# A fused attention and FFN kernel on one core: ten products of a cleared tile at the head of TensorE's order, and a new table of offsets for the order

## The chip, the cores and the metric

The kernel runs on one core of one Trainium2 chip. The metric is the device time of one execution in microseconds (us), the median of three runs. A core has TensorE (matrix products into the eight banks of PSUM), VectorE, ScalarE, GpSimd and SyncE, which here does nothing but issue DMAs. Each engine takes its instructions in the order in which the program lists them; semaphores hold an instruction until what it needs is there. In rows, PE is TensorE, PEld its weight loads, DVE VectorE, ACT ScalarE, POOL GpSimd, SPq SyncE's queue.

## What is computed

```python
def _attn_ref(q, k, v):                       # 8 batches, 12 heads, 448 positions, 64 columns
    scores = scale * np.matmul(q, k.transpose(0, 1, 3, 2)) - np.log(S)
    attn = 1.0 / (1.0 + np.exp(-scores))      # a sigmoid, no softmax
    return np.matmul(attn, v)

def _moe_ref(x, U, V, w_ch1, w_ch2):          # x: 8 x 448 x 768
    h = x.transpose(0, 2, 1) @ U @ V          # mixing over positions, rank 32
    u = x + h.transpose(0, 2, 1)
    ch = np.maximum(u @ w_ch1, 0.0) @ w_ch2   # 768 -> 3072 -> 768
    return u + ch
```

q, k and v are float32; U, V, w_ch1 and w_ch2 arrive as 64-bit floats and are decoded on the chip.

## The kernel before

**Stages.** Heads are taken in pairs, six pairs p per batch b. For each pair `S{b}{p}` on TensorE is a step of scores, ScalarE makes the sigmoid, `V{b}{p}` is the product with v, VectorE copies it out. After pairs 3 and 5, a half of the mixing follows: `M{b}{h}` (scale, split into two fp16 parts, transposes, product with U) and `N{b}{h}` (product with V, added to x, maximum of each row). `P{b}` splits u into two fp16 parts. The 64-bit weights come in pieces of 768 KB: `D{i}{g}` loads and decodes the four pieces of group g of matrix i (VectorE shifts and ors, ScalarE takes absolute sums), `E{i}{g}` splits them into two fp16 parts, `w__90` and the like. The FFN of batches 0 and 1 is plain: `I{b}{g}{f}` is one bank of 18 products of w1 with u, `O{b}{g}{e}` 12 products of w2. Batches 2 to 7 go in pairs by seven products of quarter matrices (`X`, `Y`, line L1209), whose sums `Q`, `R`, `T` are made ahead of time while the plain FFN runs. Float32 products stand for scores and values of most batches and cost two records each in the trace.

**What sets the order.** No instruction is placed by hand. Every step is recorded in a `Plan` with its engine, an assumed cost, what it reads and writes, the buffers that it needs and a position. `Plan.order` then goes through assumed time: of the steps that an engine could start, the one with the least position is next. Positions are worked out from some thirty constants (`START`, `ROOM`, `LEAD`, ...), and `SHIFT` has an offset for each group of steps and engine: `S13` moves the scores of pair 3 of batch 1, `L13s` their loads on SyncE (the trailing s). The program then has each engine's steps in that order. So a new number in `SHIFT` can move a step on its engine past any other that it doesn't depend on. Positions set the order alone; what a step waits for on the chip is set by semaphores.

**Names at the start.** `qk__99`, `qk__100` and `qk__101` hold q and k of a pair (two halves of 64 partitions each, so four loads), `v__102` to `v__105` hold v. `w` in a load from `w_in` is a piece of 64-bit weights. `junk` is a tile that ScalarE's absolute sums write to. The scores' line is L637 (L641 for the quarter of the positions that two pairs share, the quad tile), values L656 and L666, the load helper L460.

Of the kernel before, what the change touches and what calls it, by code (L numbers as in the profile page):

```python
# [71 lines left out]
MIX_2, EV_IN, EV_OUT, A_OFF = 4.517, 103.098, 7.053, -86.824
START, DECODE = 429.303, 176.054
U_AT, U_STEP = 18.398, 14.623
LEAD, SUMS, STEP_K, STEP_I, FFN_LEAD = -24.08, 276.154, 211.52, 183.044, -43.857
W_AT, W_STEP, PAIR0, MIX0A, MIX0B, W2_LAG, G0_LEAD = -168.245, 57.904, 30.158, 55.287, -54.095, 1.409, -15.896
LOW_G = 1
FB = 8
SHIFT = dict(
    mixing=-7.5, mixings=44.1, L00s=48.8, S00=92.2, V00=15.1, L01s=31, S01=63.5, V01=29.3, L02s=22.2, S02=45.5, V02=48.8, L03s=71.1, S03=90.8,  # L80
# [3 lines left out]
    D02=-10, E02=-11.3, E02s=-12.7, D12s=10.6, D12=31.3, E12=-11.2, E12s=-46.2, I020=33.2, O010=31.8, I021=6.4, O011=-35.7, I022=20.1, I023=14.7,
    O012=26, D03s=42.2, D03=28.2, E03=-30.4, E03s=20.9, D13s=-31.5, D13=-3.3, E13=13.4, E13s=-16, I030=48.6, O020=-73.1, I031=30.7, O021=-3.1,
    I032=36.4, I033=50, O022=16.1, D04s=-27.8, D04=1.2, E04=8.4, E04s=17.7, D14s=-59.4, D14=-19.9, E14=21, E14s=75.7, I040=-31.9, O030=-62.5,
    I041=-13, O031=-121.4, I042=-20.1, I043=22.8, O032=-110.2, D05s=-45.9, D05=13.7, E05=-54, E05s=-6.1, D15s=22.3, D15=15.2, E15=64.4, E15s=10,
    I050=2.9, O040=-70.1, I051=-25.7, O041=-77.1, I052=-55.7, I053=-67.8, O042=-96.4, L10s=87, S10=-28, V10=-47.5, L11s=59.7, S11=-18.1, V11=-16.8,
    L12s=79.5, S12=-26.7, V12=31.5, L13s=69.3, S13=-51.1, V13=41.4, M10=21.6, M10s=86.6, N10=-5.2, N10s=-56.2, L14s=51.6, S14=20.7, V14=16.7,
    L15s=80.7, S15=-15.9, V15=69.1, M11=14.1, M11s=185.1, N11=50.9, N11s=-94.5, P1=-23.4, P1s=5.3, L20s=94.9, S20=-29.9, V20=82.6, L21s=70.2,  # L90
    S21=11.8, V21=46.8, L22s=101.4, S22=-6.6, V22=79.8, L23s=112.5, S23=-11.3, V23=94.4, M20=24.5, M20s=-35.5, N20=-23.8, N20s=5.8, L24s=104.9,
    S24=-18.9, V24=95.2, L25s=108.1, S25=-11.6, V25=69.4, M21=-10.6, M21s=-39.5, N21=15.7, N21s=13.2, L30s=70.4, S30=-17.8, V30=-49.2, L31s=66.8,
    S31=2.2, V31=-47.6, L32s=92.9, S32=-6.8, V32=-107.6, L33s=79.2, S33=2.4, V33=-62.9, M30=17.4, M30s=-31.5, N30=33.9, N30s=-52.7, L34s=60.7,
    S34=-12.1, V34=-62.7, L35s=89.5, S35=-11.3, V35=-56.7, M31=-3.5, M31s=-77.6, N31=-8.3, N31s=6.3, L40s=71.9, S40=-21.7, S40s=-45.8, V40=60.4,
    L41s=61.1, S41=-21.5, S41s=-47.5, V41=85.2, L42s=83.1, S42=-27.8, S42s=-11, V42=45, L43s=76.9, S43=-21, S43s=-0.3, V43=31.2, M40=-2.5, M40s=-38.8,
    N40=14, N40s=5.2, L44s=56.8, S44=7.5, S44s=-21.3, V44=-23.3, L45s=93.6, S45=-6.8, S45s=3.5, V45=22.3, M41=-35.2, M41s=13.2, N41=16, N41s=-91.7,
    L50s=69.1, S50=-19.2, S50s=-17.3, V50=-61.5, L51s=78.6, S51=-40.2, S51s=-40.5, V51=-19.7, L52s=59.9, S52=-41, S52s=-26.2, V52=32.2, L53s=58.3,
    S53=-54.5, S53s=-12.6, V53=-13.7, M50=24.4, M50s=-31.2, N50=10.9, N50s=-20.7, L54s=50.5, S54=-1.2, S54s=-33.1, V54=-52.7, L55s=57.8, S55=-15.8,
    S55s=-47, V55=-57.8, M51=9.2, M51s=-35.7, N51=-30.8, N51s=34.5, L60s=-38.6, S60=-15.2, S60s=17.5, V60=31.7, L61s=22.4, S61=-1.9, S61s=5.6,
    V61=47.1, L62s=17.1, S62=-16.1, S62s=-12.5, V62=47.9, L63s=-15.4, S63=-19.7, S63s=-22.6, V63=43, M60=-38.9, M60s=59.8, N60=-2.5, N60s=-3.1,  # L100
    L64s=2.2, S64=-28.5, S64s=-22.4, V64=33.3, L65s=9.6, S65=2, S65s=-21.5, V65=58.6, M61=17, M61s=8.9, N61=27.9, N61s=-65.4, L70s=-27.4, S70=33.8,
    V70=6.9, L71s=-29.1, S71=22.1, V71=35.8, L72s=-49.3, S72=37.5, V72=42.5, L73s=-23.3, S73=34.4, V73=-19.4, M70=-39, M70s=-48.6, N70=8.2,
    N70s=-34.9, L74s=-6.2, S74=39, V74=35.5, L75s=-41.2, S75=54.5, V75=-1, M71=-85, M71s=-10.8, N71=18.9, N71s=-13.6, U1s=-69.2, U1=65.3, G1s=-57.1,
    F010s=6, F110s=-39.9, Q000=36.2, Q000s=-44.7, Q001=42.4, Q001s=-49.8, Q100=-52.3, Q100s=-58.6, Q101=-20.6, Q101s=33.5, I100=26.4, O050=-4.5,
    O050s=12.7, I101=-16.8, O051=-11.1, O051s=1.9, I102=3.3, I103=-13.2, O052=-17, O052s=-8.6, F011s=-4.2, F111s=5.3, Q010=17.8, Q010s=-55.8, Q011=11,
    Q011s=23.9, Q110=27.4, Q110s=31.2, Q111=-13.3, Q111s=23.3, I110=9.7, O100=10.9, I111=-56.7, O101=25.1, I112=-51.7, I113=-72.3, O102=34.3,
    F012s=83.4, F112s=-61.4, Q020=-20.6, Q020s=47.1, Q021=22.4, Q021s=49, Q120=3.6, Q120s=-35.8, Q121=-31.4, Q121s=-24.9, I120=-22.5, O110=40.2,
# [1366 lines left out]
```

## Time and profile before

| | us |
|---|---|
| median of three runs | 1526.42 |
| lowest and highest | 1525.07, 1526.78 |
| the profiled execution, own time | 1523.58 |
| its span, first to last instruction | 1521.8 |
| TensorE busy | 1504.0 |
| VectorE busy | 1072.8 |
| ScalarE busy | 668.1 |
| GpSimd busy | 301.3 |
| mean DMA rate | 199 GB/s |

The span is what rows are timed in, from its start. An engine's busy time is the union of its instructions; matmuls overlap in the records, so the sum of their durations is more than the time that they take. A wait is idle time of an engine in front of an instruction, with what ended it.

### The profile page before, as it was taken

What the parts mean: (1) busy time and instruction counts of PE and PEld (TensorE: products, weight loads), DVE (VectorE), ACT (ScalarE), POOL (GpSimd) and SP (SyncE); (2) the same over time, 40 slices, a digit from 0 to 9 for tenths busy, and PEclk for the clock granted to TensorE, in tenths of its full rate; (3) what the DMA queues carried; (4) which work ended last, traced back from release to release, by engine and by line L of the source; (5) the groups of instructions that cost most, each with busy time, mean ns of one, the idle gap of its engine ahead of it and who ended that gap; (6) DMA issues with size and microseconds to landing.
All of it is one profiled execution on the core that took longest, in us unless ns stands there. A gap on an engine that the chain in (4) does not pass through costs nothing.

```text
span 1521.8 us, 21953 instructions
## 1 busy us (share of the span) xinstructions
PE 1504.0 (99%) x8181; PEld 724.1 (48%) x8181; DVE 1072.8 (70%) x1822; ACT 668.1 (44%) x1058; POOL 301.3 (20%) x355
## 2 busy tenths in 40 slices
PE   8899999999999999999999999999999999999998
PEld 3344444444444444445555555555555555555554
DVE  5898998876667776658767777765665767475564
ACT  5767767855545655525233461322222432141120
POOL 0100000046656610003454461000000500000000
PEclk9999999999999999999999999999999999999999
DMA  8769998988976886795666676444253565433331
GB/s 231 241 194 294 300 292 262 348 245 251 262 166 170 254 246 184 243 293 198 233 227 219 202 252 208 151 133 124 74 166 108 179 210 162 138 112 121 107 101 73
DMA packets 209116, 303.41 MB, mean 199 GB/s; under 512 B 58096, under 2 KB 165872, under 8 KB 205936
## 3 DMA queue, kind: packets, MB, share of 16 engines
q1 hardware_dynamic: 209008, 302.00, 64.1%
q8 instruction: 64, 1.05, 0.3%
q14 instruction: 44, 0.36, 0.1%
HBM read 227.70 MB, written 64.60 MB: 192 GB/s over the span
## 4 chain that ended last, share of the span: by engine, by line
PE 92%; DMA 4%; DVE 2%; ACT 1%; SPq 0%; issue 0%; POOL 0%; ACTq 0%
PE banks L1209 55%; PE banks L1001 10%; PE banks L1021 10%; PE banks L656 6%; PE banks L637 6%; DMA w<-w_in 1%; PE banks L666 1%; PE banks L641 1%; PE banks L911 1%; DMA w__90<-kept 1%; DMA v__102<-v_in 1%; DMA stg<-ufar 0%; PE banks L921 0%; DMA xst<-xst 0%; SPq L460 0%; DVE us__88 L492 0%
## 5 line engine op out<-in xcount | busy, mean ns | idle before, releaser
L1209 PEld LDWEIGHTS <-w__93 128*128 128x128 f16 x1260 | 123.3, 98 | 114.9
L1209 PEld LDWEIGHTS <-w__92 128*128 128x128 f16 x1197 | 117.1, 98 | 109.3
L1209 PEld LDWEIGHTS <-w__91 128*128 128x128 f16 x1134 | 111.0, 98 | 103.4
L1209 PEld LDWEIGHTS <-w__90 128*128 128x128 f16 x945 | 92.4, 98 | 86.8 <-issue 0.7
L765 ACT ACTIVATE a<-banks,bias_s 128x896 f32<-128x896 f32 x105 | 99.9, 1002 | 30.0 <-PE banks L637 30.0
L1065 POOL TENSOR_TENSOR w<-w 128x384 f32<-128x384 f32 x96 | 104.6, 1089 | 5.0
L1001 PE MATMUL banks<-us__88,w__90 128*128 128x448 f16 x432 | 85.6, 353 | 1.8 <-DMA w__90<-kept 0.7
L1001 PE MATMUL banks<-us__88,w__91 128*128 128x448 f16 x432 | 85.3, 353 | 0.0
L1021 PEld LDWEIGHTS <-w__92 128*128 128x128 f16 x504 | 47.8, 98 | 53.4 <-issue 11.0
L1061 POOL TENSOR_TENSOR w<-w 128x384 f32<-128x384 f16 x48 | 44.7, 962 | 121.5 <-DVE xnt L1073 88.6
L1209 PE MATMUL banks<-a,w__92 128*128 128x448 f16 x282 | 65.1, 352 | 0.0
L1001 PEld LDWEIGHTS <-w__90 128*128 128x128 f16 x432 | 41.3, 98 | 45.0 <-issue 6.8
L1001 PEld LDWEIGHTS <-w__91 128*128 128x128 f16 x432 | 41.5, 98 | 42.5 <-issue 5.6
L1209 PE MATMUL banks<-a,w__93 128*128 128x448 f16 x279 | 61.6, 352 | 0.0
L1072 ACT CAST xnt<-w 128x1536 f16<-128x1536 f32 x24 | 35.3, 1469 | 52.2 <-POOL w L1065 52.2
L1021 PE MATMUL banks<-h__95,w__92 128*128 128x448 f16 x288 | 57.9, 353 | 0.0
L1209 PE MATMUL banks<-a,w__91 128*128 128x448 f16 x249 | 56.4, 352 | 0.0
L1166 POOL TENSOR_TENSOR stg<-h__94,w 128x448 f32<-128x448 f32 x1 | 1.1, 1147 | 264.7 <-DVE ub__86 L492 264.7
L1021 PEld LDWEIGHTS <-w__93 128*128 128x128 f16 x360 | 33.9, 98 | 38.0 <-issue 8.4
L492 DVE SCALAR_TENSOR_TENSOR stg<-w,stg 128x768 int32<-128x768 int32 (+1 forms) x49 | 46.3, 948 | 4.0 <-ACT stg L543 3.3
L492 DVE SCALAR_TENSOR_TENSOR t<-w,t 128x768 int32<-128x768 int32 (+2 forms) x51 | 47.0, 927 | 2.9 <-ACT t L543 1.9
L1073 DVE TENSOR_TENSOR xnt<-w,xnt 128x1536 f16<-128x1536 f32 x24 | 42.0, 1751 | 3.7 <-ACT xnt L1072 3.6
(1309 smaller groups left out, 3241.2 us busy)
## 6 DMA issues: line engine op xcount, KB each, us to landing
w<-w_in SPq DMA_DIRECT2D x48, 768.0 KB, 6.5
forms<-xnt SPq DMA_DIRECT2D x24, 768.0 KB, 4.7
w__93<-forms SPq DMA_DIRECT2D x20, 768.0 KB, 5.7
w__92<-forms SPq DMA_DIRECT2D x19, 768.0 KB, 5.1
w__91<-forms SPq DMA_DIRECT2D x18, 768.0 KB, 5.2
w__90<-forms SPq DMA_DIRECT2D x15, 768.0 KB, 6.0
w<-kept SPq DMA_DIRECT2D x12, 768.0 KB, 5.2
w__92<-kept SPq DMA_DIRECT2D x43, 192.0 KB, 2.9
```

What stands on the lines that cost most here:

```text
L492: nc.vector.scalar_tensor_tensor(out=out, in0=in0, scalar=s, in1=in1, op0=op0, op1=op1)
L637: nc.tensor.matmul(sc[j].x[:, h, :S], x[rows_of(h), j * P : j * P + P], y[rows_of(h)], start=i == 0, stop=i == n - 1)
L641: nc.tensor.matmul(sc[j].x[rows_of(m), h, :S], x[rows_of(h), 3 * P : S], y[rows_of(h)], start=i == 0, stop=i == n - 1)
L656: nc.tensor.matmul(av.x[rows_of(h), :S], x[:, j, rows_of(h)], y(tiles[j], h), start=j == 0 and i == 0, stop=not quad and j == 2 and i == n ...
L765: act(cost, lambda: nc.scalar.activation(out_(), in_(), AF.Sigmoid, bias=bias_s, scale=c if ws else by.x), kin + ["bias"] + ([] if ws else ...
L1001: nc.tensor.matmul(ph.x[:, :S], w.x[:, f, c, x], us.x[:, c, y, :], start=c == 0 and i == 0, stop=c == NP - 1 and i == 2,)
L1021: nc.tensor.matmul(po.x[:, :S], w.x[:, f, e, x], h.x[:, f, y, :], start=f == 0 and i == 0, stop=f == FC - 1 and i == 2,)
L1061: pool(0.87, lambda j=j: nc.gpsimd.tensor_tensor(out=t.x[:, j], in0=quarter(j, 0), in1=quarter(j, 1), op=ALU.add), [w] if b is None else k ...
L1065: pool(1.0, lambda o_=o_, x=x, y=y, sub=sub: nc.gpsimd.tensor_tensor(out=t.x[:, o_], in0=t.x[:, x], in1=t.x[:, y], op=ALU.subtract if sub ...
L1072: act(1.45, lambda: nc.scalar.copy(made(0), t.x.rearrange(order)), [(t, j) for j in range(4)], [(o, 0)], pos)
L1073: dve2(1.75, lambda: nc.vector.tensor_tensor(out=made(1), in0=t.x.rearrange(order), in1=made(0), op=ALU.subtract), [(t, j) for j in range( ...
L1209: nc.tensor.matmul(bank.x[:, :S], wt[1](k, n, x), both(f)[:, y], start=start and k == i == 0, stop=k == 2 and i == 2, skip_group_check=True)
```

## The change

Ahead of everything VectorE clears `junk`, and TensorE multiplies it by itself ten times (`WARM = 10`), into one bank that nobody reads. Both steps have a position of -1e4, so they are the first that their engines take up. The plan counts 0.378 us for each product. All but a few of the constants and all of `SHIFT` are replaced by other numbers. No other step is added, removed or changed.

```diff
-ROOM0, ROOM, AHEAD, BEFORE, PACE = 398.521, 296.816, -43.658, 258.265, 0.788
+ROOM0, ROOM, AHEAD, BEFORE, PACE = 392.306, 347.61, -109.014, 221.218, 0.657
 TURN = 1
+WARM = 10
 HOLD = 0.15
-UV_AT = -3.074
-LATER_AT = 104.309
...
-    mixing=-7.5, mixings=44.1, L00s=48.8, S00=92.2, V00=15.1, L01s=31, S01=63.5, V01=29.3, L02s=22.2, S02=45.5, V02=48.8, L03s=71.1, S03=90.8,
...
+    mixing=19.4, mixings=50.9, L00s=59, S00=48, V00=23.5, L01s=39.8, S01=28.7, V01=38.3, L02s=23.1, S02=8.4, V02=33.5, L03s=71.4, S03=49.6, V03=47.9,
...
     def mixing():
+        plan.group = "mixing"
+        dve(0.2, lambda: nc.vector.memset(junk, 0.0), (), ["still"], -1e4)
+        plan.group = None
+        first = plan.tile("first", BANK, False)
+
+        def idle():
+            for _ in range(WARM):
+                nc.tensor.matmul(first.x[:, :S], junk[:, :P], junk[:, :S], start=True, stop=True)
+
+        pe(0.378 * WARM, idle, ["still"], [first], -1e4)
         plan.group = "mixing"
```

What the table does to the order is seen in the built programs. On TensorE the scores of pair 1 (`S01`, six products in the program) now stand ahead of the values of pair 0 (`V00`), behind which they stood; up to the first mixing that engine's order is else the same. Lines of the changed kernel are 1 to 11 higher than those of before (L461 for L460).

The head of SyncE's queue, before: q and k of pair 0, v, then the first piece of `w1_in`.

```order
L460 DMA qk0__99<-k_in 64x448
L460 DMA qk0__99<-q_in 64x448
L460 DMA qk0__99<-k_in 64x448
L460 DMA qk0__99<-q_in 64x448
L460 DMA v0__102<-v_in 128x512
L460 DMA w64_107<-w1_in 128x6x128
L460 DMA qk1__100<-k_in 64x448
```

The same head now:

```order
L461 DMA w64_107<-w1_in 128x6x128
L461 DMA qk0__99<-k_in 64x448
L461 DMA qk0__99<-q_in 64x448
L461 DMA qk0__99<-k_in 64x448
L461 DMA qk0__99<-q_in 64x448
L461 DMA v0__102<-v_in 128x512
L461 DMA qk1__100<-k_in 64x448
```

The weight piece has moved from the sixth place to the first, past q, k and v of pair 0.

Further on in SyncE's queue the pieces of group 1 of w1 (`D01`) stand between the loads of batch 1's first pairs. Before:

```order
L460 DMA qk1__100<-k_in 64x448
L460 DMA qk1__100<-q_in 64x448
L460 DMA qk2__101<-k_in 64x448
L460 DMA qk2__101<-q_in 64x448
L460 DMA qk2__101<-k_in 64x448
L460 DMA qk2__101<-q_in 64x448
L460 DMA v0__102<-v_in 128x512
L460 DMA v2__104<-v_in 128x512
L460 DMA w64_107<-w1_in 128x6x128 x3
```

Now:

```order
L461 DMA qk1__100<-k_in 64x448
L461 DMA qk1__100<-q_in 64x448
L461 DMA w64_107<-w1_in 128x6x128
L461 DMA qk2__101<-k_in 64x448
L461 DMA qk2__101<-q_in 64x448
L461 DMA qk2__101<-k_in 64x448
L461 DMA v0__102<-v_in 128x512
L461 DMA v2__104<-v_in 128x512
L461 DMA qk2__101<-q_in 64x448
L461 DMA w64_107<-w1_in 128x6x128 x2
```

One of the three pieces has gone six loads up.

VectorE in front of the first FFN product: the splits of u into fp16 (`us0__88`), copies of batch 1's values (`ub2__84`), decoding steps on `stg_109`, splits of group 1 of w1 (`w01__91`). Before, from the fourth split on:

```order
L492 SCALAR_TENSOR_TENSOR us0__88<-ua3__79,s_u0__179,us0__88 128x448
L492 SCALAR_TENSOR_TENSOR us0__88<-ua4__80,s_u0__179,us0__88 128x448
L492 SCALAR_TENSOR_TENSOR us0__88<-ua5__81,s_u0__179,us0__88 128x448
L811 COPY ub2__84<-banks_110 128x448
L558 TENSOR_REDUCE mx10__200<-ub2__84 128x1
L811 COPY ub3__85<-banks_110 128x448
```

Now:

```order
L493 SCALAR_TENSOR_TENSOR us0__88<-ua3__79,s_u0__179,us0__88 128x448
L493 SCALAR_TENSOR_TENSOR stg_109<-w64_107,stg_109 128x768
L493 SCALAR_TENSOR_TENSOR w01__91<-t32_89,s_w1__198,w01__91 128x6x128
L822 COPY ub2__84<-banks_110 128x448
L493 SCALAR_TENSOR_TENSOR us0__88<-ua5__81,s_u0__179,us0__88 128x448
L559 TENSOR_REDUCE mx10__200<-ub2__84 128x1
```

A decoding step, a split of w1 and a copy now come before the last split of u; a second decoding step moved up past the first (it stands before the splits of u). On TensorE one step of scores of pair 5 of batch 1 moved ahead of the first FFN product.

Last, SyncE's queue around the load of w1's group 4 for batch 1 (`w00__90` from `kept0_146`). Before:

```order
L460 DMA qk0__99<-k_in 64x448
L460 DMA qk0__99<-q_in 64x448
L460 DMA w00__90<-kept0_146 128x6144
L893 DMA_TRANSPOSE xst_108<-xst_108 128x21x128
L460 DMA qk2__101<-k_in 64x448
```

Now:

```order
L904 DMA_TRANSPOSE xst_108<-xst_108 128x21x128
L461 DMA row0__111<-far2_1_116 128x256
L461 DMA qk0__99<-k_in 64x448
L461 DMA qk0__99<-q_in 64x448
L461 DMA qk0__99<-k_in 64x448
L461 DMA qk0__99<-q_in 64x448
L461 DMA qk2__101<-k_in 64x448
L461 DMA qk2__101<-q_in 64x448
L461 DMA qk2__101<-k_in 64x448
L461 DMA qk2__101<-q_in 64x448
L461 DMA w00__90<-kept0_146 128x6144
```

The load has gone behind the transposing DMA of batch 5's first mixing half and behind the four loads of `qk2__101`. On TensorE the product that reads it (`I140`) has gone behind `V55`, one mixing product step of `M50` and three of `N50`, and the scale of `M50` has gone ahead of `V54` and `I133`.

## Rows read from the trace of the kernel before

**Rows 1.** The page: busy us of each engine, share of the span, instructions.

```profile
PE 1504.0 (99%) x8181; PEld 724.1 (48%) x8181; DVE 1072.8 (70%) x1822; ACT 668.1 (44%) x1058; POOL 301.3 (20%) x355
```

**Rows 2.** Busy time by stage: the stretch, its length, then busy us (and instructions) of PE, PEld, DVE, ACT and POOL, granted clock, DMA share, GB/s.

```profile
30.00:60.00 30.00, 25.66 (x144) 8.73 (x141) 23.38 (x46) 19.19 (x26) 5.59 (x5) 1.00 0.87 268
60.00:90.00 30.00, 27.65 (x166) 12.12 (x163) 28.69 (x55) 25.43 (x35) 4.05 (x4) 1.00 0.68 197
...
120.00:200.00 80.00, 78.53 (x414) 33.67 (x411) 72.90 (x129) 61.25 (x92) 5.69 (x5) 1.00 0.96 301
200.00:508.00 308.00, 307.56 (x1779) 137.88 (x1777) 229.28 (x403) 188.67 (x291) 116.48 (x156) 1.00 0.85 247
508.00:700.00 192.00, 191.26 (x1094) 84.85 (x1095) 131.63 (x254) 97.58 (x152) 32.17 (x45) 1.00 0.85 249
```

**Rows 3.** The start: the chain of waits (start us, us, what), and behind it the line of the stretch 0 to 16.5 us in the table by stage.

```profile
4.26 6.08 PE banks L637 x12
10.34 2.63 PE banks L656 x12
12.97 2.46 PE banks L637 x12
15.43 0.91 PE banks L641 x8
...
0.00:16.50 16.50, 12.23 (x46) 5.40 (x48) 2.70 (x4) 7.53 (x9) 1.22 (x9) 1.00 0.84 236
```

**Rows 4.** SyncE's queue at the start: issues in the timeline (start us, us), the weight load of the second half of pair 0, and, from the list of DMAs in narrow stretches, KB and us from issue to landing of the first half of pair 0, the first w piece, the first v and the last half of pair 1.

```profile
0.72 0.59 SPq L460 DMA_DIRECT2D qk__99<-k_in  x1
3.27 0.59 SPq L460 DMA_DIRECT2D v__102<-v_in  x1
3.90 0.61 SPq L460 DMA_DIRECT2D w<-w_in  x1
5.49 0.73 PEld L637 LDWEIGHTS banks<-qk__99 64*128 64x128 f32 x4 [0.76 <-issue]
6.53 0.59 SPq L460 DMA_DIRECT2D qk__100<-q_in  x1
...
qk__99<-k_in SPq DMA_DIRECT2D x1, 112.0 KB, 2.5
w<-w_in SPq DMA_DIRECT2D x1, 768.0 KB, 5.4
v__102<-v_in SPq DMA_DIRECT2D x1, 256.0 KB, 3.0
qk__100<-q_in SPq DMA_DIRECT2D x1, 112.0 KB, 4.9
```

**Rows 5.** Between 18 and 59 us: timeline of VectorE, TensorE and ScalarE (start us, us; in brackets idle time before and what ended it), and the D01 load in the chain of waits.

```profile
18.33 0.56 DVE L489 TENSOR_SCALAR stg<-w 128x768 int32<-128x768 int32 x1 [6.48 <-DMA w<-w_in]
38.18 0.97 PE L666 MATMUL banks<-a,v__102 64*64 64x448 f32 x4 [0.97 <-DMA v__102<-v_in]
43.56 7.45 DMA w<-w_in
51.12 1.02 ACT L543 ACTIVATE t<-w,minus 128x768 f32<-128x768 uint16 x1 [4.96 <-DMA w<-w_in]
53.09 0.97 PE L656 MATMUL banks<-a,v__102 128*64 128x448 f32 x4 [0.73 <-ACT a L765]
58.40 0.34 PE L901 MATMUL banks<-ident,us__88 128*128 128x128 f16 x3 [1.22 <-ACT us__88 L890]
```

**Rows 6.** Between 63 and 88 us: timeline of TensorE and VectorE, and (the first line) a group of VectorE's instructions of 60 to 90 us, busy us and mean ns.

```profile
L492 DVE SCALAR_TENSOR_TENSOR stg<-w,stg 128x768 int32<-128x768 int32 x4 | 3.8, 954 | 0.1
...
67.77 0.74 PE L921 MATMUL banks<-vst,t 128*128 128x448 f16 x3 [1.32 <-DVE t L492]
68.44 1.77 PE L637 MATMUL banks<-qk__101 64*128 64x448 f32 x8
86.15 0.61 DVE L811 COPY ub__84<-banks 128x448 f32<-128x448 f32 x1
86.81 3.58 PE L1001 MATMUL banks<-us__88,w__90 128*128 128x448 f16 x18 [0.23 <-DVE ub__84 L811]
```

**Rows 7.** Steps of eighteen FFN products in the chain, without and with a change of tile mode ahead of them.

```profile
190.38 3.40 PE banks L1001 x18
...
238.69 3.51 PE banks L1001 x18
```

**Rows 8.** Around 508 us: SyncE's issues and TensorE in the timeline, and the weight fetch in the chain of waits.

```profile
500.31 0.58 SPq L460 DMA_DIRECT2D w__90<-kept  x1
503.78 4.73 SPq L893 DMA_TRANSPOSE xst<-xst  x1
...
500.31 7.88 DMA w__90<-kept
...
508.23 3.58 PE L1001 MATMUL banks<-us__88,w__90 128*128 128x448 f16 x18 [0.67 <-DMA w__90<-kept]
511.74 2.48 PE L656 MATMUL banks<-a,v__102 128*64 128x448 f32 x12
516.21 3.57 PE L1001 MATMUL banks<-us__88,w__90 128*128 128x448 f16 x18
519.62 0.73 PE L921 MATMUL banks<-vst,t 128*128 128x448 f16 x3
```

More of the change, by code (lines that the diff above doesn't have):

```diff
@@ L63 @@
 PIPE, LANDS, LATE = 0.32e6, 3.237, 0.155
-ROOM0, ROOM, AHEAD, BEFORE, PACE = 398.521, 296.816, -43.658, 258.265, 0.788
+ROOM0, ROOM, AHEAD, BEFORE, PACE = 392.306, 347.61, -109.014, 221.218, 0.657
 TURN = 1
+WARM = 10
 HOLD = 0.15
-UV_AT = -3.074
-LATER_AT = 104.309
-PREP, BOUNDS, VALUES, SECOND, MIXED = 49.161, 81.976, -3.762, 7.022, 1.69
+UV_AT = -33.896
+LATER_AT = 83.917
+PREP, BOUNDS, VALUES, SECOND, MIXED = 44.287, 60.266, -3.913, 5.616, -1.226
 MIXED1, MIX_1 = 6.273, 55.569
[L72 to L76, printed above, removed]
+MIX_2, EV_IN, EV_OUT, A_OFF = 46.788, 90.213, 0.234, -86.824
+START, DECODE = 389.191, 164.285
+U_AT, U_STEP = 22.896, 9.968
+LEAD, SUMS, STEP_K, STEP_I, FFN_LEAD = 10.771, 230.851, 166.789, 171.929, -43.857
+W_AT, W_STEP, PAIR0, MIX0A, MIX0B, W2_LAG, G0_LEAD = -171.485, 53.207, 25.979, 30.467, 0.462, 1.361, -13.62
 LOW_G = 1
@@ L84 @@
[L84 to L107, printed above, removed]
@@ new lines @@
+    E00=-56.9, E00s=-29.2, D10s=-63.7, D10=5.6, E10=-26.9, E10s=18.3, I000=-6.3, I001=-44.9, I002=-40.9, I003=-1.7, D01s=-47.3, D01=-60.5, E01=-36.6,
+    E01s=-73.1, D11s=-36.6, D11=-18.2, E11=33.5, E11s=-25.1, I010=-68.2, O000=-54.3, I011=34.7, O001=-11.8, I012=6.5, I013=-52.4, O002=-2.1,
+    D02s=-68.1, D02=-21, E02=-19.4, E02s=-4.6, D12s=17.6, D12=25.9, E12=-53, E12s=-74.4, I020=11.9, O010=21.6, I021=-18.9, O011=-32.8, I022=18.6,
+    I023=6.4, O012=36.1, D03s=25.6, D03=8.9, E03=-42.3, E03s=4.1, D13s=-34, D13=5.6, E13=31.7, E13s=-25.4, I030=56.2, O020=-74.2, I031=32.3,
@@ new lines @@
+    S35=-4.1, V35=-37.9, M31=1.7, M31s=-60.6, N31=-18.5, N31s=-13.2, L40s=75.2, S40=-2.7, S40s=-58.3, V40=68.8, L41s=65, S41=-11.6, S41s=-49.2,
+    V41=63.8, L42s=96.7, S42=-27.8, S42s=-27, V42=47.2, L43s=73.1, S43=-11.8, S43s=-34.8, V43=25.1, M40=18.9, M40s=-22.4, N40=20.9, N40s=7.5,
+    L44s=52.4, S44=16.7, S44s=-51.7, V44=-44, L45s=98.2, S45=-5.6, S45s=-14.7, V45=26.9, M41=-31.4, M41s=-1.2, N41=21.9, N41s=-99.7, L50s=72.4,
+    S50=-25.7, S50s=-18.2, V50=-63.9, L51s=69.5, S51=-31.3, S51s=-31.7, V51=-11.3, L52s=60.3, S52=-51, S52s=-23, V52=48, L53s=55.1, S53=-64.1,
@@ new lines @@
+    G6s=-9.2, G7s=-28.6, X60s=16.8, X60=34, X61s=-42, X61=-64.4, X62s=-47.5, X62=-81, X63s=88.4, X63=127.3, Y600s=-75.6, Y600=35.3, X64s=58.9,
+    X64=1.3, Y601s=-31.5, Y601=-7.7, Y602s=25.5, Y602=-17.2, X65s=-104.1, X65=-46.3, X66s=5.3, X66=-16.3, Y610s=-8.6, Y610=-25.7, X67s=-16.7,
+    X67=-25.3, Y611s=1.8, Y611=-7.6, Y612s=24.4, Y612=-71.8, X68s=-6.3, X68=29.6, X69s=43.7, X69=68.6, Y620s=23.6, Y620=32.7, X610s=-17.3, X610=-3.2,
+    Y621s=-7.2, Y621=44, Y622s=18.2, Y622=62.6, X611s=15.7, X611=-27.7, Y630s=79.4, Y630=20.1, Y631s=14.1, Y631=14.8, Y632s=15.6, Y632=61.7
```

54 lines of the change are left out of this document (33 added, 21 removed).

## Prediction

> **What bounds the kernel now.** I read the page first: TensorE is busy in 1504.0 of 1521.8 us [rows 1]. A busy TensorE can still be a slow one, so I asked the chain for its pace: eighteen products of 448 columns take 3.40 us, 0.189 us each, and 3.51 where the tile mode (64 or 32 rows instead of 128) changed just before them [rows 7]. So little is left inside the products. What can be won lies in the time before the first product, in the first products, and in TensorE's waits.
>
> The table by stage gives the waits, as the stretch less TensorE's busy time [rows 2]: 4.34 us from 30 to 60, 2.35 from 60 to 90, 1.47 from 120 to 200, 0.44 up to 508, 0.74 up to 700. The timeline dates the larger ones: 0.97 at 38.18, ended by a v load, 0.73 at 53.09, ended by ScalarE, 1.22 at 58.40, ScalarE again [rows 5], 1.32 at 67.77, VectorE [rows 6]. The reader is to see that none is ended by TensorE's own earlier work. Having TensorE ready earlier ahead of them only lengthens them; having it later, by up to the sum of 6.7 us, shortens them.
>
> The first products are slow. In the chain the twelve records of pair 0's scores take 6.08 us and the twelve of pair 1, of the same form, 2.46; the values behind the first take 2.63 [rows 3]. The granted clock reads 1.00 for this stretch [rows 3], but I take the durations to show the lower of TensorE's two levels, 1.2 instead of 2.4 GHz, up to some 10.5 us. The loss is 6.08 - 2.46 = 3.6 us, and 0.2 in the values: 3.8 us, 0.25% of the time, the most that a raised clock can give.
>
> **The change, step by step.** *The ten products.* The clear is one VectorE instruction, which no row shows; between nothing and VectorE's first decoding step on 128x768, 0.56 us [rows 5]. SyncE's first issue is at 0.72 [rows 4], which I take for the others' start too, so products begin between 0.7 and 1.3. They cost 0.189 us each at the full level [rows 7], twice that at the lower, so 1.9 to 3.8 us for ten, and end between 2.6 and 5.1.
>
> *What the order does to q and k.* The first load on SyncE's queue is now a 768 KB piece of w1, ahead of the four halves of q and k. In the trace, loads of this queue land in the order of issue: v, issued 3.27, lands 3.0 later, at 6.3; the piece behind it, issued 3.90, 5.4 later, at 9.3; the last of pair 1's four halves, issued 6.53, 4.9 later, at 11.4 [rows 4]. So the piece takes 3.0 us of the queue and a half (11.4 - 9.3) / 4 = 0.53. A half that is first in the queue lands 2.5 us after its issue at 0.72 [rows 4]. With the piece first, it lands at 0.72 + 2.5 + (3.0 - 0.53) = 5.7, and pair 0's halves at 6.2, 6.75, 7.3 and 7.8. The products are over by then and cost nothing themselves, but pair 0's scores begin 2.5 us later than the 4.26 of now, behind 1.6 us of idle TensorE or more.
>
> At the full level the three score tiles take 2.46 us behind the last half at 7.8: 10.3, against 10.34 now. Next in the new order are pair 1's scores, not pair 0's values. Their halves have the same loads ahead of them as before and land at 11.4, or up to 0.5 sooner; scores to 13.9, values to 16.3, the quad tile (0.91 [rows 3]) to 17.2. Now it ends at 15.43 + 0.91 = 16.34. **So even with the clock up TensorE is 0.4 to 0.9 us later here**: the queue takes what the clock gives. At the lower level the three tiles take 10.34 - 5.49 = 4.85 us from the second half on [rows 3, 4]: 12.65 and, by the same steps at a level that rises as late after the first score as it does now, 18.7, so 2.4 us late. The waits of 6.7 us that follow take in either. I count 0, with 0 to +1 for the range.
>
> The Trainium skill (TensorE: Matmul & The Clock Gate, Why this matters for your kernels) warns against idle gaps of TensorE between bursts, since a long one drops the clock again. It speaks against the gap behind the products; by it the case of 2.4 us would hold. The nearest row agrees only in part: behind the 1.32 us gap at 67.77 three products take 0.74, as many as the three without a gap at 519.62, 0.73 [rows 6, 8]; no row shows a gap of 1.6 us ahead of products.
>
> *The first w piece early.* VectorE gets it at 5.7 instead of 9.3. Behind its decoding VectorE waits 6.48 us for the next piece [rows 5], so this is worth nothing.
>
> *The first piece of D01 early.* Its load goes six loads up. Issued at 43.56, it landed 7.45 later; ScalarE idled 4.96 us for it, with its conversion at 51.12 in front of the sigmoid that holds TensorE to 53.09 [rows 5]. At 0.6 us for an issue [rows 4] it comes up to 3.6 us sooner. That takes away at least the 0.73 us there; ScalarE's splits at 58.40 stand behind the same work and can come sooner by up to 0.73 + 1.0, the second an idle conversion's place. I take 1.7, because ScalarE's idle time is larger than that.
>
> *VectorE before the first FFN product.* From 60 to 90 VectorE is busy 28.69 of 30 us [rows 2]: it sets the time. In its new order four more steps stand ahead of the last split of u that the product at 86.81 needs: two decoding steps and one split of w1 at 0.95, one copy of values at 0.61 [rows 6], together 3.5 us. On TensorE one more step of scores (eight records, 1.77 us [rows 6]) stands ahead of that product and covers half of it. With the 1.7 us from above: 3.5 - 1.8 - 1.7 = 0. Bounds: no early gain at all, +1.7; VectorE's four steps in gaps that it has, 30 - 28.69 = 1.3 us, -1.3.
>
> *Tile modes.* Going through both orders I count 211 changes of mode before and 207 after; at 3.51 - 3.40 = 0.11 us each, -0.4.
>
> *The later waits,* 1.47 + 0.44 + 0.74 = 2.65 us: the order around each is new; between -2.65 and as much more I take 0.
>
> Sum: 0 + 0 - 0.4 = -0.4 us on the profiled execution (1523.58, span 1521.8). That one lies 2.8 below the median of 1526.42, and I carry the difference over: **1526.0 us, no change**. What a measurement of this kernel can tell from no change is 0.2%, 3.05 us.
>
> **The rivals.** *The clock is paid out* (0.32). For it: 3.8 us are really lost at the start, and a new order may close waits too. Against it: q and k come late, and the waits don't pass TensorE's time on. If the 3.8 get through and a quarter of the 6.7 us goes: 1526.4 - 3.8 - 1.7 - 0.4 = 1520.5.
>
> *The products don't raise the clock* (0.15, inside no change). Then 2.4 us are lost at 17 us and the waits take them in; if they took in none, 1528.4.
>
> *A weight fetch comes late* (0.21), which ends slower. At 508.23 the first product of FFN group 4 of batch 1 waits 0.67 us for its weights, issued 500.31, landed 7.88 later [rows 8]. In the new order this load stands behind the transposing DMA, which holds SyncE for 4.73 us, and behind four halves into `qk__101`; the four into `qk__99` were ahead of it before, but not of the transpose. Eight issues of 0.6 us [rows 4] are 4.8. TensorE gets there later too, by a values step and seven mixing products (511.74 to 516.21, 4.5) and three more (0.6): 508.23 - 0.67 + 5.1 = 512.7. If the transpose stays at 503.78: 503.78 + 4.73 + 4.8 + 7.88 = 521.2, a wait of 8.5 instead of 0.67, 1533.8. If it moves up by the FFN step and the values step that its scaling now passes on TensorE, 3.4 + 2.5 = 5.9 [rows 7, 3]: 515.3, a wait of 2.6, 1527.9. It decides (more than 3.05 us) if the fetch is issued after 512.7 - 7.88 + 0.67 + 3.05 = 508.5. Between the two I put 1531. Against it: the lag of 7.88 has other transfers in it, and the half as large piece at 3.90 needed 5.4 [rows 4].
>
> **Numbers.** No change 0.47 (around 1526.0, itself 1523.4 to 1529.4), faster 0.32, slower 0.21. For 8 in 10 the range reaches into both: down to 1520.0, just past the paid-out clock, and up to 1531.0, the middle of the late fetch.
>
> **What would show it.** In the changed profile: ten products from about 1 us on; first scores near 6.8 (wrong if near 4.3 to 5.1), their twelve records in about 3.5 us with the wait for the last halves in it, or 6 if the clock stayed low; the quad tile's end near 17.2; no wait at 53, the wait at 38 still there, shorter; the first FFN product near 88.6; at most a short wait near 512. I am wrong if TensorE's waits between 30 and 90 shrink by more than 3 us together while the start stays as it was, or if that fetch holds TensorE for more than 4.

## The result, and the profile after

The changed kernel takes 1534.08 us (median of five, 1532.31 to 1535.37) against 1526.42 (1525.07 to 1527.44): ratio 1.0051, 95% interval 1.0037 to 1.0066. It is slower by 7.7 us, outside the range given; the rival of the late weight fetch came nearest in time, but the loss lies elsewhere. The profiled execution has 1535.37 us and a span of 1533.6, 11.8 more than the one before; some 4 of these are chance, for the profiled execution of before lay 2.8 us under its median and this one lies 1.3 over its own.

The table by stage of the changed kernel (columns as in [rows 2]):

```profile
0.00:30.00 30.00, 26.48 (x120) 10.22 (x120) 12.96 (x30) 15.90 (x19) 1.22 (x9) 0.94 0.82 223
30.00:60.00 30.00, 26.46 (x139) 8.73 (x131) 22.03 (x43) 18.60 (x24) 5.90 (x5) 1.00 0.88 245
60.00:90.00 30.00, 27.55 (x168) 12.36 (x169) 28.36 (x54) 25.89 (x37) 4.89 (x5) 1.00 0.73 224
120.00:200.00 80.00, 79.33 (x419) 35.34 (x418) 74.72 (x132) 59.86 (x90) 4.32 (x5) 1.00 0.90 293
200.00:508.00 308.00, 308.00 (x1782) 137.79 (x1780) 232.59 (x404) 189.64 (x296) 118.75 (x150) 1.00 0.85 249
508.00:700.00 192.00, 191.16 (x1092) 84.49 (x1091) 135.12 (x257) 98.48 (x148) 36.31 (x50) 1.00 0.87 254
700.00:1000.00 300.00, 291.34 (x1527) 149.56 (x1525) 233.01 (x327) 104.41 (x171) 123.41 (x113) 0.99 0.59 198
```

and the same stretch of the kernel before, which [rows 2] do not have:

```profile
700.00:1000.00 300.00, 300.00 (x1588) 155.19 (x1586) 226.17 (x343) 110.22 (x182) 113.37 (x112) 1.00 0.62 208
```

Up to 700 us TensorE's idle time is much as in [rows 2] (3.54 and 2.45 us from 30 to 90, where it had 4.34 and 2.35; 0.67, 0 and 0.84 later, where it had 1.47, 0.44 and 0.74). From 700 to 1000 us, where it never waited before, 300 - 291.34 = 8.66 us are new. TensorE's longer waits there, by what ended them (us in total, times, longest):

```profile
PE banks L1220 <- DVE a L493: 3.2, 1, 3.2
PE banks L1220 <- DVE ub__85 L493: 1.7, 1, 1.7
PE banks L1220 <- DVE v__105 L1259: 1.4, 1, 1.4
PE banks L1220 <- DVE a L1259: 1.0, 1, 1.0
PE banks L1220 <- DVE xst L493: 0.7, 1, 0.7
PE banks L1220 <- DVE us__88 L493: 0.4, 1, 0.4
```

All of these are on VectorE, which is far from full (233 of 300 us); 0.2 us on ScalarE are the rest. Behind the longest the timeline of TensorE and a narrow stretch of the table show a second loss, the half clock:

```profile
854.60 5.25 PE L1220 MATMUL banks<-a,w__93 128*128 128x448 f16 x18 [3.20 <-DVE a L493]
```

```profile
855.00:859.00 4.00, 4.00 (x14) 1.71 (x13) 2.77 (x5) 1.11 (x2) 0.00 (x0) 0.57 0.20 59
```

Eighteen products took 3.57 us in the same place of a run without that wait (below), so 1.68 more. 8.66 + 1.68 = 10.3 of the 11.8 us lie between 700 and 1000 us.

Why VectorE is late is in its timeline ahead of 854 us, with GpSimd's beside it (start us, us):

```profile
840.43 1.76 DVE L1084 TENSOR_TENSOR xnt<-w,xnt 128x1536 f16<-128x1536 f32 x1
842.64 0.68 DVE L493 SCALAR_TENSOR_TENSOR us__88<-banks,fg,h__94 128x448 f32<-128x448 f32 x1
844.76 1.33 DVE L493 SCALAR_TENSOR_TENSOR us__88<-us__88 128x448 f32<-128x448 f32 x1
846.02 1.33 DVE L493 SCALAR_TENSOR_TENSOR t<-us__88,w 128x448 f32<-128x448 f32 x1
847.27 1.42 DVE L1259 TENSOR_TENSOR h__95<-w,h__95 128x448 f16<-128x448 f32 x1
848.61 1.42 DVE L1259 TENSOR_TENSOR xst<-us__88,xst 128x448 f16<-128x448 f32 x1
849.94 1.42 DVE L1259 TENSOR_TENSOR a<-t,a 128x448 f16<-128x448 f32 x1
851.28 1.41 DVE L493 SCALAR_TENSOR_TENSOR t<-v__102,t 128x448 f32<-128x448 f32 x1
852.62 0.67 DVE L493 SCALAR_TENSOR_TENSOR xst<-banks,fg,h__94 128x448 f32<-128x448 f32 x1
853.32 0.62 DVE L1259 TENSOR_TENSOR v__105<-t,v__105 128x448 f16<-128x448 f32 x1
...
842.26 4.60 POOL L1072 TENSOR_TENSOR w<-w 128x384 f32<-128x384 f16 x4 [4.08 <-DVE xnt L1084]
846.83 5.39 POOL L1076 TENSOR_TENSOR w<-w 128x384 f32<-128x384 f32 x4
```

SBUF is the memory on the chip in which the tiles lie; `banks` are PSUM. Six steps of the group X28, whose two inputs lie in SBUF, take 1.33 to 1.42 us each while GpSimd makes the quarter sums of a weight piece (Q051); one more, ahead of them at 844.05, took 0.79. The same kind of step takes 0.62 once GpSimd is done at 852.22. The step with an input in a PSUM bank that falls beside the sums (842.64) keeps its 0.68. GpSimd started there because VectorE's `xnt` step freed its tile. The kernel before has the same two groups, in another order:

```profile
837.22 1.75 DVE L1073 TENSOR_TENSOR xnt<-w,xnt 128x1536 f16<-128x1536 f32 x1
841.75 0.68 DVE L492 SCALAR_TENSOR_TENSOR w<-banks,fg,t 128x448 f32<-128x448 f32 x1 [1.02 <-PE banks L1209]
844.05 1.34 DVE L492 SCALAR_TENSOR_TENSOR us__88<-xst,us__88 128x448 f16<-128x448 f32 x1
849.69 0.62 DVE L492 SCALAR_TENSOR_TENSOR h__95<-a,h__95 128x448 f32<-128x448 f32 x1
852.32 0.62 DVE L1248 TENSOR_TENSOR w<-h__95,w 128x448 f16<-128x448 f32 x1
...
839.10 3.78 POOL L1061 TENSOR_TENSOR w<-w 128x384 f32<-128x384 f16 x4 [6.74 <-DVE xnt L1073]
842.85 4.75 POOL L1065 TENSOR_TENSOR w<-w 128x384 f32<-128x384 f32 x4
```

There most steps beside the sums read banks. Three SBUF steps began beside them (1.34, 0.82 and 0.71 us, the last at 847.37); those from 849.16 on, when GpSimd was through (847.6), took 0.61 to 0.62. Counted over the timeline from 690 to 1010 us, VectorE steps on 128x448 of 0.95 to 1.6 us ("long steps") number 13 before and 37 after; none of them reads a bank.

The planner knows of this. It books GpSimd's reads and VectorE's two-input steps (those with `port`) one behind the other:

```
now.append((max(free[e], ready[i], r[0] + o[5] if r[1] else 0.0, port if o[8] else 0.0, landed[-8] if e == "SP" else 0.0), o[4] - bond, i))
...
if o[8]:
    port = end[i]
```

In its order X28's run of steps stands between two of Q051's sums. But that is a time in its plan. On the chip nothing made GpSimd wait for that run, and both went as soon as their inputs were there.

### The profile page after: what moved, and what is told of

The parts are those of the page before. It is cut to its first block, busy times and chain, and to the rows that moved or that the text cites. A ratio compares the mean times of both kernels' runs of the same rounds, so it can differ in the third digit from the quotient of the medians.

```text
span 1533.6 us, 21966 instructions
## 1 busy us (share of the span) xinstructions
PE 1509.6 (98%) x8191; PEld 725.8 (47%) x8191; DVE 1097.9 (72%) x1823; ACT 669.1 (44%) x1059; POOL 321.7 (21%) x355
## 4 chain that ended last, share of the span: by engine, by line
PE 86%; DVE 8%; DMA 3%; ACT 1%; issue 1%; POOL 0%; SPq 0%; ACTq 0%; POOLq 0%; DVEq 0%
PE banks L1220 52%; PE banks L1012 10%; PE banks L1032 9%; PE banks L667 6%; PE banks L648 6%; PE banks L677 1%; DMA v__102<-v_in 1%; PE banks L652 1%; PE banks L922 1%; DVE stg L493 1%; DVE us__88 L493 1%; DVE t L493 1%; DMA w<-w_in 0%; PE banks L932 0%; DMA xst<-xst 0%
## 5 line engine op out<-in xcount | busy, mean ns | idle before, releaser
L1220 PE MATMUL banks<-a,w__90 128*128 128x448 f16 x348 | 80.2, 352 | 0.0
L1220 PE MATMUL banks<-a,w__93 128*128 128x448 f16 x324 | 74.7, 359 | 4.2 <-DVE a L493 3.2
L1220 PE MATMUL banks<-a,w__91 128*128 128x448 f16 x240 | 54.5, 352 | 0.4 <-DVE us__88 L493 0.4
L493 DVE SCALAR_TENSOR_TENSOR stg<-w,stg 128x768 int32<-128x768 int32 x48 | 45.9, 962 | 3.7 <-ACT stg L544 2.8
L493 DVE SCALAR_TENSOR_TENSOR t<-w,t 128x768 int32<-128x768 int32 (+1 forms) x50 | 46.1, 927 | 1.1 <-ACT t L544 0.3
```

The costliest lines, as they stand in the source:

```text
L493: nc.vector.scalar_tensor_tensor(out=out, in0=in0, scalar=s, in1=in1, op0=op0, op1=op1)
L1220: nc.tensor.matmul(bank.x[:, :S], wt[1](k, n, x), both(f)[:, y], start=start and k == i == 0, stop=k == 2 and i == 2, skip_group_check=True)
```

## The experiments

**Theory A:** the new order lets VectorE's steps with two SBUF inputs meet GpSimd's reads; they shut each other out, and VectorE, in order, is late for TensorE. **Rivals:** B, the products or the start cost it; C, the order of VectorE's steps and of the banks does, with GpSimd only near; D, the late stage is right and what comes before leaves it late; E, GpSimd's results come late, by its occupancy. Results are given as the median time in us, the ratio to runs of the kernel before on the same chip, and in brackets the 95% interval of the ratio. "Missed" means that the result lies outside what was expected. In runs that say so the weights of the late stage are not the true ones; the order of work is kept unless the text says otherwise.

**The products.** Left out of the changed kernel, and put alone at the head of the kernel before:

```diff
-            self.ops[i][2]()
+            if i > 1:                       # first kernel
+                self.ops[i][2]()
...
+        nc.vector.memset(junk, 0.0)         # second kernel, ahead of plan.emit()
+        for _ in range(10):
+            nc.tensor.matmul(BANK[0].ap[:, :S], junk[:, :P], junk[:, :S], start=True, stop=True)
```

> The changed kernel with its order kept, but the clearing step and the ten products left out. Theory A (the loss lies in the stage from 700 to 1000 us, where VectorE's steps with two inputs in SBUF meet GpSimd's sums in the new order): 1532 to 1537 us, ratio to the kernel before 1.004 to 1.007, and 6 to 10 us of TensorE's waits from 700 to 1000 us again. Rival B (the products themselves cost it, by a clock that falls later or by the start): back at 1525 to 1528, waits of 700 to 1000 us under 2 us.

> The kernel before with its order kept, and the clearing step and ten products put ahead of everything. Theory A: 1524 to 1527.5 us (ratio 0.998 to 1.001), no waits of TensorE from 700 to 1000 us. Rival B (the products cost it): 1530 or more.

Without them: 1535.97 us, 1.0056 [1.0036, 1.0076], 37 long steps, the same waits behind 700 us. Alone: 1526.42, 0.9994 [0.9979, 1.0008], 13 long steps, no wait there. B falls. The products do their work at the start; in the kernel before q and k come at once behind them, and pair 0's scores run at the full level (6.08 us in [rows 3]):

```profile
1.17 3.91 PE L1423 MATMUL banks<-junk 128*128 128x448 bf16 x10 [1.17 <-DVE junk L1421]
5.01 2.84 PE L637 MATMUL banks<-qk__99 64*128 64x448 f32 x12
```

The ten products themselves took 0.39 us each, twice the 0.189 of the full level [rows 7], so they ran at the lower one, though the clock column reads 1.00 there. The quad tile ended at 15.30 in this run, 1.0 us sooner than in [rows 3], but no gain can be measured at the end; in its trace the first FFN product begins at 88.09, in that of before at 86.81.

**Fewer columns, more sums.** Sixteen operations of Q051 and Q150 on 48 instead of 384 columns in the changed kernel (part of two late weight pieces is stale); and in the kernel before eight more sums beside X28:

```diff
+        m = P // 8 if plan.group in ('Q051', 'Q150') else P
-            pool(0.87, lambda j=j: nc.gpsimd.tensor_tensor(out=t.x[:, j], in0=quarter(j, 0), in1=quarter(j, 1), op=ALU.add),
+            pool(0.87, lambda j=j: nc.gpsimd.tensor_tensor(out=t.x[:, j, :, :m], in0=quarter(j, 0)[:, :, :m], in1=quarter(j, 1)[:, :, :m], op=ALU.add),
...
+            if self.ops[i][0] == "POOL" and self.ops[i][10] == "Q051":
+                self.sums += 1
+                if self.sums == 8:
+                    t = self.ops[i][7][0].x
+                    for _ in range(8):
+                        self.nc.gpsimd.tensor_tensor(out=self.spare, in0=t[:, 0], in1=t[:, 1], op=ALU.add)
```

> The changed kernel, order kept; GpSimd's sixteen operations of the groups Q051 and Q150 (at 842 to 874 us) work on 48 columns instead of 384, so that the later weights hold stale data there. Theory A: the 3.2 us wait at X29 (854.6 us) and the half clock behind it go, 1528 to 1530.5 us (4 to 5.5 us less than the changed kernel), and the six steps of X28 take 0.62 to 0.68 us instead of 1.33 to 1.42. Rival C (the order of VectorE's steps and of the banks is what makes TensorE wait, GpSimd is only near): the wait stays over 2 us and the time at 1533 to 1535.

> The kernel before, order kept, with eight more sums of 128x384 on GpSimd that nobody reads, right behind the eight of Q051 (from 847.6 us on, beside VectorE's steps of X28 and X29). Theory A: those SBUF steps of VectorE that meet them take 1.3 to 1.4 us instead of 0.62, VectorE comes 3 to 5 us late, and TensorE, which did not wait from 700 to 1000 us, waits 1 to 5 us there: 1527.5 to 1532 us. Rival C: no new wait, 1525 to 1527.5.

The first took 1531.75, 1.0022 [1.0011, 1.0033]: X28's six steps at 0.61 to 0.71, the 3.2 us wait gone, 30 long steps left. In ratios that is 0.29% or 4.4 us less than the changed kernel, as expected, though the time itself lies above the 1528 to 1530.5 given (the kernel before took 1527.85 on that chip). The second took 1530.5, 1.0018 [1.0005, 1.0031]; long steps rise from 13 to 19. VectorE and GpSimd in its timeline, and the longer of the two waits that follow (the other, 0.9 us, is for ScalarE):

```profile
852.93 0.68 DVE L498 SCALAR_TENSOR_TENSOR a<-banks,fg,us__88 128x448 f32<-128x448 f32 x1 [0.48 <-PE banks L1215]
853.53 1.33 DVE L498 SCALAR_TENSOR_TENSOR h__94<-a,xst 128x448 f32<-128x448 f32 x1
854.79 1.41 DVE L498 SCALAR_TENSOR_TENSOR h__95<-a,h__95 128x448 f32<-128x448 f32 x1
...
851.94 10.47 POOL L295 TENSOR_TENSOR junk<-w 128x384 f16<-128x384 f32 x8
```

```profile
PE banks L1215 <- DVE us__88 L498: 1.6, 1, 1.6
```

GpSimd's work whose result nobody reads makes TensorE wait: C falls as the cause of this wait.

**Exchanging the late order.** The places of the late groups (X, Y, T, the sums of pieces 6 to 11) put back in the changed kernel, or carried into the kernel before, by 187 offsets each:

```diff
+LATE_STAGE = dict(
...
+)
+for g, x in LATE_STAGE.items():
+    SHIFT[g] = SHIFT.get(g, 0.0) + x
```

> The changed kernel with the places in the order of the late groups alone (X, Y, T, the quarter sums of the pieces 6 to 11, the late gains) put back to those of the kernel before; products, start and all up to about 650 us as changed. Theory A (the loss is in the late stage's order, through meetings of VectorE and GpSimd): 1524 to 1528.5 us, ratio 0.998 to 1.0015, waits of TensorE from 700 to 1000 us under 2 us, some 10 to 18 long SBUF steps of VectorE there, not 37. Rival D (the loss comes from what the start and the middle leave late): 1532 or more.

> The kernel before with the places of the same late groups taken from the changed kernel; nothing else changed, no products. Theory A: 1530 to 1536 us, waits of TensorE from 700 to 1000 us of 4 to 10 us, 25 to 40 long steps of VectorE. Rival D: 1525 to 1528.

Both missed: 1541.73, 1.0085 [1.0058, 1.0111], and 1544.55, 1.0101 [1.0078, 1.0124], slower than either parent. Long steps: 29 and 19. The second waits 11.0 us at one place, for ScalarE's copies in the u forms:

```profile
PE banks L1231 <- ACT a L1191: 11.0, 1, 11.0
```

In the second, then, a group comes late for another reason; the first waits 3.7 us at each of two places for VectorE, and why VectorE was late there is open. So neither run tells A from D; runs without GpSimd's reads do (below).

**The w piece behind v.** In the changed kernel the first w1 piece (768 KB in the trace) behind pair 0's q, k and first half of v:

```diff
-        for i in self.order():
+        order = self.order()
+        order.remove(214)
+        order.insert(order.index(42) + 1, 214)
+        for i in order:
```

> The changed kernel, order kept, but the first 0.92 MB piece of w1 is fetched behind pair 0's q, k and first half of v instead of ahead of them. If the late start (the quad tile ended at 18.18 us against 16.34 before) goes on to the end: 1531 to 1532.5 us, the quad ends 1 to 2 us earlier. If later waits for loads take it up, as the prediction has it: 1533 to 1535.5 us, though the quad ends 1 to 2 us earlier; the waits from 700 to 1000 us stay at 7 to 10 us.

Missed: the quad tile ended later, at 22.82 instead of 18.18. Pair 0's scores ran at once, from 5.01, but the next product in this order is pair 1's score, and its q and k stood behind the w piece now; a wait for a sigmoid followed:

```profile
10.38 0.99 PE L651 MATMUL banks<-qk__100 64*128 64x448 f32 x2 [1.69 <-DMA qk__100<-q_in]
15.12 3.36 PE L651 MATMUL banks<-qk__100 64*128 64x448 f32 x8 [2.60 <-ACT a L779]
```

1538.43 us, 1.0066 [1.0043, 1.0090], which holds the 1.0051 of the changed kernel. Of the 4.6 us lost at 20 us some 2 are left at the end by the medians; the interval allows for none and for all. The waits from 700 to 1000 us stay (8.7 us).

**GpSimd without reads.** In the changed kernel the operations of pieces 6 to 11 and T40 to T42 become clears (and sums of 48 columns); those weights and forms are zero or stale. The control does the same to the kernel before. Then clears that fill the time, three for each operation, or two and a small one:

```diff
-            pool(0.87, lambda j=j: nc.gpsimd.tensor_tensor(out=t.x[:, j], in0=quarter(j, 0), in1=quarter(j, 1), op=ALU.add),
+            pool(0.87, lambda j=j: clear(t.x[:, j]) if g > 2 else nc.gpsimd.tensor_tensor(out=t.x[:, j], in0=quarter(j, 0), in1=quarter(j, 1), op=ALU.add),
...
+    def clear(x):
+        for _ in range(2):
+            nc.gpsimd.memset(x, 0.0)
+        nc.gpsimd.memset(x[:, 0, :32] if len(x.shape) == 3 else x[:, :32], 0.0)
...
```

> The changed kernel, order kept; GpSimd's operations of the weight pieces 6 to 11 and of T40 to T42 are replaced by clears of the same tiles, which read nothing, and by sums of 48 columns, so that those weights and u forms are zero or stale. Theory A: every wait of TensorE from 700 to 1000 us goes (8.66 us, under 1.5 left) with the half clock behind the longest, 1523 to 1527.5 us; VectorE's steps there take 0.62 to 0.68 us. Rival C (the order of VectorE's steps has its own share): 3 us or more of those waits stay, 1528 to 1532.

> The kernel before, order kept, with the same replacement as the changed kernel had in the run with few clears (pieces 6 to 11 and T40 to T42: clears and sums of 48 columns). Theory A: there were 13 long steps of VectorE and no wait of TensorE from 700 to 1000 us to be had back, so 1525 to 1528.5 us, ratio 0.998 to 1.001. Rival (GpSimd's work costs the kernel before as much): 1519 to 1523.

> The changed kernel, order kept; each of GpSimd's operations of the weight pieces 6 to 11 and of T40 to T42 is replaced by three clears of the tile that it wrote, so that GpSimd is occupied as long or longer (110 to 140 us from 700 to 1000 us) and holds its results back as long, but reads nothing; those weights and u forms are zero. Theory A (what costs is that VectorE's steps with two inputs in SBUF and GpSimd's reads shut each other out): the waits of 700 to 1000 us go as in the run with few clears, under 1.5 us left, 1523 to 1528 us, VectorE's steps at 0.62 to 0.68 us. Rival E (GpSimd's results come late for VectorE and TensorE, whatever it does meanwhile): 5 us or more of the waits stay, 1530 to 1535.

> As the run with three clears for each operation of GpSimd, but with two clears and one of 32 columns, so that a group of eight operations takes 7 to 8 us, as it does undisturbed in the changed kernel, instead of 10.56. Theory A (the long steps cost it: VectorE's two SBUF inputs against GpSimd's reads): under 2.5 us of TensorE's waits from 700 to 1000 us are left, 1523 to 1528.5 us (ratio 0.997 to 1.001). Rival E (GpSimd's occupancy costs it): 5 us or more of waits, 1530 to 1536.

Few clears: 1524.75, 0.9977 [0.9964, 0.9990], no long step, no wait from 700 to 1000 us:

```profile
700.00:1000.00 300.00, 300.00 (x1587) 155.19 (x1586) 211.24 (x340) 109.09 (x181) 38.78 (x106) 1.00 0.63 206
```

The control: 1526.57, 1.0003 [0.9986, 1.0020]; the kernel before had nothing to win. With the changed start and middle untouched the loss is gone, so D falls. Three clears missed: 1535.63, 1.0048 [1.0032, 1.0063], not one long step, but 7.5 us of waits:

```profile
PE banks L1224 <- DVE a L493: 2.6, 1, 2.6
PE banks L1224 <- ACT xst L1248: 2.6, 1, 2.6
PE banks L1224 <- POOL xst L1055: 2.3, 1, 2.3
```

The clears were too long. GpSimd was busy 150.9 us from 700 to 1000, against 123.4, a group took 10.56 us, and VectorE stood idle for 4.42 us in front of its `xnt` step, which by way of ScalarE's conversion has to wait for such a group. So E is real once GpSimd has more to do than it had. With clears of matched length it is not what the changed kernel suffers from: 1524.22 us, 0.9980 [0.9969, 0.9991]. The table by stage and the timeline:

```profile
700.00:1000.00 300.00, 300.00 (x1588) 155.17 (x1587) 207.63 (x326) 109.13 (x181) 112.94 (x363) 1.00 0.63 207
```

```profile
844.56 0.62 DVE L1264 TENSOR_TENSOR xst<-us__88,xst 128x448 f16<-128x448 f32 x1
844.64 0.90 POOL L1055 MEMSET w<- 128x384 f32 x2
```

GpSimd works 112.9 us there and nothing waits, neither VectorE's steps nor TensorE.

**Holding GpSimd.** The whole computation, with the plan's order made a real one: GpSimd reads 16 columns of the last step of VectorE's run before it goes on. One place (Q051 behind X28), then 13 places (runs of four steps or more), then 19 (three or more, T60 to T62 too). For the one place (the numbers are steps of the plan):

```diff
+        held, last = (2743, 2744, 2745), 3197
+        order = [i for i in order if i not in held]
+        order[order.index(last) + 1 : order.index(last) + 1] = held
...
+            if i == last:
+                x = self.ops[i][7][1].x.bitcast(F16)[:, S : S + 16]
+                self.nc.gpsimd.tensor_tensor(out=self.junk[:, :16].bitcast(F16), in0=x, in1=x, op=ALU.add)
```

> The changed kernel with its whole computation; GpSimd's sums of Q051 are held behind the last VectorE step of X28 by a sum of 16 columns that reads that step's output, and the order of the other engines is kept. Theory A: X28's six long steps take 0.62 to 0.7 us again, the 3.2 us wait at 854.6 us and the half clock behind it go, 1528 to 1531 us (ratio 1.000 to 1.003), unless the sums, now at 849 to 857 us, meet X29's steps instead, which would give 1 to 2 us of it back. Rival C: 1533 to 1535.

> The changed kernel with its whole computation; wherever the plan's order puts four or more two-input steps of VectorE between two operations of GpSimd on the weight pieces 6 to 11 and on T40 to T42 (13 places), GpSimd is held behind the last of them by a sum of 16 columns that reads its output. Theory A: 15 to 30 long steps instead of 37, of TensorE's waits from 700 to 1000 us 1 to 4 us are left, 1524.5 to 1530 us (ratio 0.998 to 1.003), at the lower end only if the held sums don't make u forms or weights late. Rival E: held GpSimd is later still, so 1532 to 1540.

> As the run with 13 holds of GpSimd, but a hold wherever three or more two-input steps of VectorE stand between two of its operations, and on T60 to T62 too (19 holds). Theory A with the slack read from the trace (no wait of TensorE was left from 700 to 1300 us in the run with 13 holds, so that fewer long steps buy nothing): 1523.5 to 1526.5 us, ratio 0.997 to 1.000, as with 13. If long steps cost beyond TensorE's waits: 1521 to 1523.

One hold: 1530.58, 1.0029 [1.0013, 1.0045]. The sums come behind X28, and the eighteen products run on without a wait at the full level:

```profile
847.12 0.21 POOL L297 TENSOR_TENSOR junk<-v__105 128x16 f16<-128x16 f16 x1 [11.04 <-DVE v__105 L1266]
847.29 3.52 POOL L1079 TENSOR_TENSOR w<-w 128x384 f32<-128x384 f16 x4
849.13 3.57 PE L1227 MATMUL banks<-a,w__93 128*128 128x448 f16 x18
```

13 holds: 1524.95, 0.9988 [0.9975, 1.0001]. 19 holds: 1524.39, 0.9981 [0.9970, 0.9991], faster than both kernels, with TensorE busy for

```profile
700.00:1000.00 300.00, 299.89 (x1587) 154.99 (x1585) 229.16 (x341) 109.95 (x180) 124.17 (x130) 1.00 0.61 207
```

18 and 21 long steps are left, and TensorE's idle time there is 0.1 us in either: a long step costs only where TensorE stands behind it. Since the whole computation is done in these runs, and GpSimd is held back in them, E falls here too.

## Why the prediction was wrong

**The late fetch of q and k** was right in kind. The first score began at 7.40 (given: 6.8), behind a wait of 2.32 us, and the quad tile ended 1.84 us later than before, between the two cases (0.4 to 0.9, and 2.4), since the clock fell in part:

```profile
7.40 4.83 PE L648 MATMUL banks<-qk__99 64*128 64x448 f32 x11 [2.32 <-DMA qk__99<-q_in]
```

```profile
8.60:11.90 3.30, 3.30 (x10) 1.84 (x11) 0.14 (x1) 2.60 (x4) 0.00 (x0) 0.50 0.97 230
12.00:16.50 4.50, 4.50 (x24) 2.19 (x22) 0.00 (x0) 4.50 (x6) 0.00 (x0) 1.00 1.02 296
```

The level was full at first, half from 8.6 to 11.9, then full: behind the gap part of what the products gave was lost. The products took 3.91 us, a little over the 1.9 to 3.8 given. The warning cited from the Trainium skill (TensorE: Matmul & The Clock Gate, Why this matters for your kernels) is of gaps between matmul bursts that are longer than this one. So it was no ground for the case of 2.4 us, as the prediction took it to be, and the fall behind 2.32 us is told by the trace alone.

**That later waits take this in** is borne out in part. Leaving out the products made the quad tile end 1.1 us later still (19.30), but the first FFN product began at 90.11, where it was 90.19, with 0.05% at the end, inside the interval. Moving the w piece made the quad tile end 4.6 us later; of that 3.1 were left at the first FFN product (93.30), and 0.15% at the end, which the interval can't tell from nothing.

**D01's early piece:** the wait at 53 is gone, as said; the one at 38, now at 40.67, is longer (2.1 us for v) where shorter was said. **VectorE ahead of the first FFN product:** 90.19, given 88.6; 86.81 before. One trace can't settle this: it began at 86.81 to 88.09 in four runs with the order of before, at 88.68 to 92.26 in nine with the changed order up to there (the two mixtures and the run with the w piece behind v left out). **The weight fetch near 512:** 0.73 us of waiting at 513.79, so this rival did not come about: the transposing DMA moved up to 496.64, and the fetch was issued at 506.95, ahead of the 508.5 from which it would have decided. **Later waits up to 700 us:** 2.65 became 0.67 + 0 + 0.84 = 1.5. **Tile modes** were not measured apart.

**The step that failed** is the term of the later waits, "between -2.65 and as much more I take 0". It was bounded by waits that the trace of before had, and ended at 700 us, because TensorE had none behind it. A new order can make waits where there were none: 10.3 us from 700 to 1000 us in the profiled execution, because VectorE's steps met GpSimd's reads. Without these waits the changed kernel stands at 0.9977 to 0.9988 of the kernel before (few clears, matched clears, 13 and 19 holds), 2 to 3.5 us faster. So the rest of the sum, -0.4 us, was too cautious by 1.5 to 3 us; which of its terms gave that is open, since executions of one kernel differ by as much as that. Which of the new offsets brought the steps and the reads together is open too.

The Trainium skill (SBUF — State Buffer, Who interferes with whom) states what these runs show: an instruction of VectorE with two inputs in SBUF contends with one of GpSimd that reads SBUF, not with one that only writes it. The runs agree: 1.33 to 1.42 us beside sums, 0.62 beside clears.

## What to carry over

Where a change re-orders everything, read the stages without a wait too: for each run of VectorE steps with two SBUF inputs, look in the trace where GpSimd's reads fall and what now stands beside them in the new order. An exclusion that this planner only books by time did not bind on the chip; a tiny read that makes one engine wait did, at 0.2 us each. And a table of offsets is to be taken as a whole: half of one and half of another was worse than both, either way round.

## What the runs showed of the hardware

A bank as one input is enough to keep a VectorE step clear of GpSimd: 73 such steps of the kernel before and 54 of the changed one, from 700 to 1000 us, lay half a microsecond or more beside a GpSimd instruction, and all took 0.66 to 0.69 us. Both engines pay where they meet: the eight sums of Q051 took 4.60 + 5.39 = 9.99 us beside X28, and 3.52 + 5.13 = 8.65 behind it, where the last four met four steps of X29 (1.18 to 1.42 us).

In the changed kernel the half level came back after TensorE had resumed, not in the wait: the wait ended at 854.60, the clock read 1.00 up to 855, then 0.57 from 855 to 859, and eighteen products cost 1.68 us more. Waits of 1.0 and 1.7 us in the same stage were not followed by one. How long the wait is does not tell by itself. The same wait of 3.20 us in the run with the w piece behind v, up to 858.82, was followed by eighteen products at the full level (3.56 us). In the run with the products alone a wait of 2.04 us, up to 510.49, was followed by the half level from the first product on (eighteen in 5.06 us).
